# Block list in one packet, masks of a second half on VectorE, split first copies and a new order of steps in a fused attention and MLP kernel

## The chip, the cores and the metric

One core of one Trainium2 chip. The metric is device time in microseconds (us). A profile's span is about 1.8 us shorter than the device time of the same execution. Engines: PE (matrix engine; PEld is its loading of weights), ACT (ScalarE), DVE (VectorE), POOL (GpSimd), SP (issues DMAs). The granted clock is the share of PE's full speed that the profile says it was given.

## The reference

Block-sparse attention (batch 4, 8 heads, 768 positions, head size 64, blocks of 32), then a two-layer MLP with exact gelu on its output:

```python
mask = |blk_i - blk_j| <= 1 or first/last block row or column or sampled_blocks[blk_i]
attn = softmax(where(mask, q k^T / 8, -1e9)) @ v          # per batch and head
x = attn as (3072, 512)
out = gelu(x @ w_in) @ w_out                              # 512 -> 2048 -> 512
```

## The kernel before

The work is cut into eight halves of a batch (384 rows). While the hidden layer and the output of one half run, the scores of the next half are computed in between. What runs when is a string of tokens per stage; each engine executes its part in exactly that order. Stages in time: OPENING (scores of half 1), FIRST (MLP of half 1, scores of half 2), SECOND, SPARSE, DENSE, SPARSE2, and so on.

```python
DENSE = """
H H G t2 u2 H H H M3 t3 u3 H K03 K02 H H O3 S0 O1 K13 K12 C10 L3 O1 C11 O2 D0 W0 S1 O3 D1 O2 W1 S2 O1 X0 K11 O1 E0 O2 C12 D2 E1 W2 S3 ... X2 Y O1 K10 O2 X3 H"""
# H hidden step, O output matmuls, S/W scores and weighted sum of a pair of heads (sparse),
# F/V the same for batch 0, X transposes x for the next hidden layer, I0..I8 small index
# computations on VectorE, t/u transposes of k/q,
# K10: GpSimd gathers the sampled key blocks for the second half of a batch (1), pair 0 of heads;
# C: the same for values,
# L: GpSimd issues four loads, G: VectorE copies of the global value rows
```

Batch 0 is computed densely and masked by a second pair of matmuls, which add -30000 to barred scores:

```python
def first_scores(hb, hp, t, masked=False):
    s1 = sc_pool.tile([P, 2, 512], F32, tag="sc", name="s1")
    c = slice(t, S, NT)
    for l, r_, first_ in ((st["k", hp], st["q", hp], True), (onehot, barred, False)):
        if masked and not first_:
            continue
        for h in range(2):
            pe.matmul(s1[:, h, 0:HALF], lhsT=l[r, c], rhs=r_[r, cq], ...)      # ... cut
    act.activation(pt, s1[:, :, 0:HALF], AF.Exp, scale=scale)
    if masked:          # exists before, but no order used it: token f
        dve.tensor_tensor(pt, pt, mask_t[:, t]..., op=ALU.mult)

def mask_tile(t):       # token m
    pe.matmul(ps[:, 0:HALF], lhsT=onehot[0:64, t:S:NT], rhs=barred[0:64, HALF:S], ...)
    dve.tensor_single_scalar(mask_t[:, t], ps[:, 0:HALF], -1.0, op=ALU.is_gt)
```

The block list is read by a DMA with a partition step of 0, so each of 128 partitions fetches the same 576 bytes:

```python
raw = msk.tile([P, NB, NR, 2], I32, name="raw")
act.dma_start(out=raw, in_=bass.AP(tensor=src, offset=0, ap=[[0, P], [1, NB * NR * 2]]))
```

The softmax here doesn't subtract the row's maximum and nothing guards it: scores larger than these inputs give would overflow.

## Time and profile before

| | before |
|---|---|
| median device time | 293.39 us (292.94 to 294.15, 4 runs) |
| span of the profiled execution | 290.4 us |
| PE busy | 265.4 us, 91% |
| mean granted clock of PE, 11 runs of a later job | 0.987 to 0.994 |

All lines of the page carry L54, a helper, so tiles and not lines tell what an instruction is: hp is the hidden layer, op the output, s scores, kg_all and v_gat gathered keys and values (and, in batch 0, exponentials that borrow their space). Busy time first, page of before:

```profile
PE 265.4 (91%) x3477; PEld 166.6 (57%) x3516; DVE 132.5 (46%) x352; ACT 163.1 (56%) x215; POOL 95.1 (33%) x134
```

PE bounds the kernel. Only its 25 idle us, stretches of low clock and removed matmuls can pay. The windows view of before: a stretch of time, then busy us and instruction count of each engine, the granted PE clock, DMA share, GB/s.

```profile
33.00:72.00 39.00, 36.88 (x395) 21.42 (x400) 26.16 (x113) 25.94 (x33) 6.27 (x14) 1.00 0.77 157
...
182.00:186.00 4.00, 0.10 (x6) 0.01 (x2) 1.31 (x3) 0.67 (x1) 1.18 (x1) 0.98 0.00 0
186.00:188.50 2.50, 2.50 (x29) 1.12 (x29) 0.56 (x1) 1.67 (x3) 0.00 (x0) 0.50 0.00 0
188.50:190.00 1.50, 1.34 (x16) 0.94 (x17) 0.57 (x1) 0.17 (x2) 0.00 (x0) 0.75 0.00 0
```

PE stands for 4 us at 182 us, and then runs at half clock. The timeline of PE in before says what it waited for (start, duration, instruction group, in brackets the idle time before it and what ended it):

```profile
181.75 0.34 PE L54 MATMUL s<-tq,tk 64*128 64x128 bf16 x6
185.99 0.48 PE L54 MATMUL s<-tq,kg_all 64*128 64x32 bf16 x22 [3.90 <-POOL kg_all L54]
186.40 0.50 PE L54 MATMUL s<-tq,kgl 128*128 128x128 bf16 x3
186.70 1.91 PE L54 MATMUL op<-w_out_sb,g 128*128 128x512 bf16 x4
```

Four output matmuls take 1.91 us; four took 1.03 us elsewhere. The timeline of POOL in before shows the other side, the end of gathers and four load issues in one queue from 150 to 186 us:

```profile
166.56 1.65 POOL L54 INDIRECT_COPY v_gat<-v_flat,idx_v 128x1024 f32 x1 [2.00 <-PE od L54]
168.15 0.80 POOL L54 DMA_DIRECT2D st<-in_k_dram  x1
...
176.95 1.18 POOL L54 INDIRECT_COPY kg_all<-tk,idx_k 128x704 f32 x1 [2.08 <-issue]
179.45 1.43 POOL L54 INDIRECT_COPY v_gat<-v_flat,idx_v 128x768 f32 x1 [1.32 <-issue]
184.75 1.18 POOL L54 INDIRECT_COPY kg_all<-tk,idx_k 128x704 f32 x1 [3.87 <-issue]
```

A key gather is busy for 1.2 to 1.6 us but comes only every 3.3 to 4.1 us: ahead of most stand 2 us or more of "issue", time in which POOL waits for nothing that the profile shows. (The profile's notes call spans on POOL rough, so a part of this may be the gather itself.) So a busy share of 33% hides a queue that is full from 150 to 186 us. The last is K10, pair 0's, which is the first that the next half's scores need.

The opening, timeline of ACT in before:

```profile
6.56 0.83 ACT L54 CAST st<-w_out_sb 128x768 bf16<-128x768 f32 x1 [4.09 <-DMA w_out_sb<-in_k_dram]
...
10.85 8.55 ACT L54 ACTIVATE kg_all<-s 128x768 bf16<-128x768 f32 x12 [1.02 <-PE s L54]
...
29.89 1.28 ACT L54 ACT_TABLE_LOAD   x1
```

k's cast waits for k until 6.56 us, the first exponential runs at 10.85 us, and the table load at 29.89 us marks the end of the 24 exponentials.

### The profile page before, as it was taken

The numbers are of one execution on the slowest core, as the hardware profiler recorded it, in microseconds if no ns is written. First come the engines' busy times: TensorE is split into PE (matmuls) and PEld (weight loads), VectorE is DVE, ScalarE is ACT, GpSimd is POOL, SyncE is SP. The second block draws the span as 40 slices with busy tenths as digits, with TensorE's granted clock in tenths as the row PEclk, the third lists the DMA queues.
The fourth block names the chain that finished last, engine by engine and source line by source line (L and its number), as shares of the span: only waits on it lengthen the run. The fifth ranks groups of instructions, "written<-read, shape, count | busy, mean of one in ns | idle before, by whom it ended". The sixth has DMA issues, their size and how long they took to land.

```text
span 290.4 us, 7951 instructions
## 1 busy us (share of the span) xinstructions
PE 265.4 (91%) x3477; PEld 166.6 (57%) x3516; DVE 132.5 (46%) x352; ACT 163.1 (56%) x215; POOL 95.1 (33%) x134
## 2 busy tenths in 40 slices
PE   0899799999999989999999999499999999999995
PEld 0566454565556755565657755266566765665544
DVE  5465585367714653274524730376633560253002
ACT  2698458764467726654576726426358546655520
POOL 8402530013353364352543474132273343100000
PEclk9999999999999999999999999799999999999999
DMA  5999999119970219387751169059100200010102
GB/s 142 266 250 210 213 229 196 50 50 242 218 122 3 74 36 165 57 212 200 164 91 38 38 107 148 0 145 248 60 2 2 74 36 2 2 52 22 40 36 72
DMA packets 30178, 31.34 MB, mean 108 GB/s; under 512 B 13664, under 2 KB 24288, under 8 KB 30144
## 3 DMA queue, kind: packets, MB, share of 16 engines
q0 software_dynamic: 11936, 13.24, 25.8%
q1 hardware_dynamic: 18064, 17.53, 23.2%
q8 instruction: 27, 0.44, 0.6%
q10 hardware_dynamic: 144, 0.07, 0.2%
q14 instruction: 7, 0.06, 0.1%
HBM read 27.34 MB, written 6.29 MB: 116 GB/s over the span
## 4 chain that ended last, share of the span: by engine, by line
PE 81%; ACT 5%; issue 5%; POOL 3%; DVE 3%; DMA 2%; ACTq 0%
PE op L54 26%; PE hp L54 25%; PE s L54 12%; PE og L54 9%; PE ps L54 4%; ACT kg_all L54 2%; PE psx L54 2%; DMA raw<-in_sampled_blocks_dram 2%; ACT g L54 2%; POOL v_gat L54 2%; PE od L54 1%; PE sd L54 1%; DVE pt_all L54 1%; POOL st L54 1%; POOL kg_all L54 1%
## 5 line engine op out<-in xcount | busy, mean ns | idle before, releaser
L54 PE MATMUL op<-w_out_sb,g 128*128 128x512 bf16 (+1 forms) x361 | 90.3, 373 | 2.3 <-issue 0.6
L54 PE MATMUL hp<-xT,w_in_sb 128*128 128x384 bf16 x512 | 88.2, 326 | 4.3 <-ACT g L54 3.8
L54 ACT ACTIVATE g<-hp 128x768 bf16<-128x768 f32 x64 | 51.0, 810 | 61.5 <-PE hp L54 61.4
L54 PEld LDWEIGHTS <-w_in_sb 128*128 128x128 bf16 x512 | 49.1, 98 | 38.2 <-issue 5.5
L54 ACT ACTIVATE pt_all<-s 128x1024 bf16<-128x1024 f32 (+2 forms) x72 | 44.2, 686 | 30.8 <-PE s L54 30.0
L54 PEld LDWEIGHTS <-g 128*128 128x128 bf16 x400 | 35.8, 98 | 29.2 <-issue 3.3
L54 POOL INDIRECT_COPY kg_all<-tk,idx_k 128x704 f32 x24 | 30.2, 1258 | 56.0 <-issue 51.5
L54 DVE TENSOR_TENSOR pt_all<-pt_all,mask_x 128x768 bf16<-128x768 bf16 x24 | 16.0, 667 | 60.1 <-ACT pt_all L54 60.1
L54 POOL INDIRECT_COPY v_gat<-v_flat,idx_v 128x1024 f32 (+1 forms) x18 | 28.6, 1591 | 41.4 <-issue 18.7
L54 PEld LDWEIGHTS <-pt_all 128*32 128x32 bf16 (+2 forms) x840 | 23.9, 101 | 6.8 <-issue 1.5
L54 DVE COPY os<-op 128x512 f32<-128x512 f32 (+1 forms) x25 | 16.6, 666 | 23.1 <-PE op L54 23.1
L54 PE MATMUL s<-tq,tk 64*128 64x128 bf16 (+1 forms) x240 | 25.7, 274 | 0.9 <-DVE tq L54 0.6
L54 PE MATMUL ps<-ident,st 128*64 128x128 bf16 x384 | 17.2, 233 | 8.3 <-ACT st L54 7.4
L54 ACT ACT_TABLE_LOAD x16 | 20.5, 1283 | 5.7 <-PE hp L54 4.2
L54 PEld LDWEIGHTS <-tk 64*128 64x128 bf16 (+1 forms) x312 | 16.2, 104 | 12.6 <-issue 5.8
L54 PEld LDWEIGHTS <-st 128*64 128x64 bf16 x384 | 12.8, 116 | 15.7 <-issue 7.5
L54 ACT ACTIVATE v_gat<-s 128x768 bf16<-128x768 f32 x24 | 18.3, 811 | 5.9 <-PE s L54 5.7
L54 ACT ACTIVATE kg_all<-s 128x768 bf16<-128x768 f32 x24 | 17.6, 819 | 2.8 <-PE s L54 2.7
L54 DVE TENSOR_TENSOR x<-og,rc 128x384 bf16<-128x384 f32 x32 | 17.8, 557 | 1.1
L54 DVE COPY tk<-ps 128x768 bf16<-128x768 bf16 x15 | 14.3, 955 | 8.4 <-PE ps L54 8.1
L54 DVE COPY tq<-ps 128x768 bf16<-128x768 bf16 (+1 forms) x16 | 14.9, 928 | 6.6 <-PE ps L54 4.9
L54 PEld LDWEIGHTS <-kg_all 64*128 64x128 bf16 (+1 forms) x672 | 14.2, 94 | 5.7 <-POOL kg_all L54 4.1
(111 smaller groups left out, 228.5 us busy)
## 6 DMA issues: line engine op xcount, KB each, us to landing
out_dram<-os SPq DMA_DIRECT2D x23, 256.0 KB, 2.3
v_flat<-v_flat SPq DMA_DIRECT2D x6, 594.0 KB, 7.0
st_v<-in_v_dram SPq DMA_DIRECT2D x12, 256.0 KB, 4.8
st<-in_k_dram POOLq DMA_DIRECT2D x7, 384.0 KB, 7.9
st<-in_q_dram POOLq DMA_DIRECT2D x7, 384.0 KB, 9.1
v_flat<-v_flat SPq DMA_DIRECT2D x6, 396.0 KB, 4.8
w_in_sb<-in_moe_w_in_dram POOLq DMA_DIRECT2D x2, 1024.0 KB, 18.0
w_out_sb<-in_moe_w_out_dram POOLq DMA_DIRECT2D x2, 1024.0 KB, 26.2
```

The source lines that it names most:

```text
L54: return self._tc.keep_in_program_order(f(*args, **kwargs))
```

## The change

Its intent: read the block list once and spread it by a matmul with ones; take the mask matmuls of 15 of 24 tiles of half 2 off PE (tokens f and m); let the first pair's copies start earlier; and set the steps in a new order around that. The transposed k of batch 0 is also kept in another order of columns.

```diff
-H H G t2 u2 H H H M3 t3 u3 H K03 K02 H H O3 S0 O1 K13 K12 C10 L3 O1 C11 ... K11 ... C12 ... K10 O2 X3 H
+M3 H H t2 u2 H H H t3 u3 H H H O2 K03 K02 O1 L3 K10 S0 O1 C10 O2 D0 O1 G O1 W0 S1 O1 K12 O2 C11 ... C12 ... K13 ... K11 O1 X1 ...
 (all other orders are rewritten too; in FIRST, m0 to m5 are added and 15 F become f)
-    raw = msk.tile([P, NB, NR, 2], I32, name="raw")
+    raw = msk.tile([1, NB, NR, 2], I32, name="raw")
-    act.dma_start(out=raw, in_=bass.AP(tensor=src, offset=0, ap=[[0, P], [1, NB * NR * 2]]))
+    act.dma_start(out=raw, in_=bass.AP(tensor=src, offset=0, ap=[[0, 1], [1, NB * NR * 2]]))
-    dve.tensor_copy(sbi, raw[:, :, :, 0])
-    dve.tensor_copy(sbf, sbi)
+    dve.tensor_copy(raw_b, raw[:, :, :, 0].rearrange("p n s -> p (n s)"))
+    pe.matmul(ps_raw, lhsT=ones, rhs=raw_b, start=True, stop=True)
+    dve.tensor_copy(sbf.rearrange("p n s -> p (n s)"), ps_raw)
@@ transpose_qk
+        if b == 0 and which == "k":                     # k of batch 0 stays in transposed order
+            to, frm, n = dst.rearrange("p (j n) -> p j n", j=NT), ps, NT
-            transpose_qk(0, hp, w, pair, (act if w == "k" else (act, dve)) if hp == 0 else dve, st)
+            transpose_qk(0, hp, w, pair, (((dve, 0, 1 / 3), (act, 1 / 3, 1)) if w == "k" else ((dve, 0, .5), (act, .5, 1)))
+                         if hp == 0 else dve, st)
```

More of the change, by code (lines that the diff above doesn't have):

```diff
@@ L59 @@
 OPENING = """
-A0 k1 F00 F01 F02 F03 F04 q1 P0 F05 F10 F11 k2 F12 q2 F13 J0 F14 F15 F20 J1 V00 V01 P1 V02 F21 k3 F22 q3 F23 F24 F25 J2 X0 F30 V10 V11 V12 F31 F32 F33 X1 V20 J3 V21 V22 F34 M1 F35 X2 V30 V31 L1 V32 H X3"""
+A0 F00 k1 F01 F02 q1 F03 F04 F05 k3 P0 F10 F11 F12 k2 q2 F13 J0 F14 F15 F20 V00 V01 V02 F21 J1 F22 q3 F23 F24 F25 X0 F30 V10 V11 V12 P1 F31 F32 J2 F33 X1 V20 V21 V22 J3 F34 M1 F35 X2 V30 V31 L1 V32 H X3"""
 FIRST = """
-I0 H H I1 H H I2 H H H I3 O1 I4 H O2 I5 O1 F00 O2 F01 F02 O1 I6 V00 F03 F04 O1 F05 O1 I7 F10 F11 V01 V02 F12 F13 O2 V10 F14 F15 O2 X0 F20 F21 O1 V11 B V12 F22 F23 t0 O1 F24 F25 u0 X1 O1 V20 V21 F30 F31 u1 V22 F32 O2 t1 F33 O2 X2 I8 F34 K00 F35 V30 O1 V31 V32 H Q1 O1 K01 Q0 R X3 O2"""
+H H m0 I0 m1 m2 I1 H H m3 m4 H I2 I3 H H I4 H O2 I5 O1 f00 O2 f01 m5 f02 O2 I6 I7 F03 F04 V00 O1 F05 f10 V01 O1 f11 V02 f12 f13 O2 f14 f15 O1 V10 O1 X0 F20 F21 u0 V11 V12 B F22 F23 V20 O1 t0 f24 f25 O1 X1 V21 O1 f30 F31 u1 V22 F32 O2 t1 f33 F34 O1 V30 f35 K00 X2 O1 I8 O1 V31 V32 Q0 O1 R Q1 H K01 X3 O2"""
@@ L63 @@
 SECOND = """
-H t2 C00 H t3 M2 u3 C01 C02 H K02 K03 u2 H H H H H K10 G O1 C10 O2 S0 C11 O3 L2 C12 O1 D0 W0 S1 E0 O2 K11 O3 K12 D1 X0 W1 S2 E1 O1 X1 O2 D2 O1 W2 S3 O1 X2 O1 E2 D3 O1 W3 E3 O3 Y K13 O1 X3 O1 H"""
+H t2 H u3 t3 C00 H C01 C02 H G H H H M2 H K02 O2 K03 S0 u2 K11 K10 C10 C11 O4 D0 O2 L2 W0 S1 O3 D1 X0 C12 O1 E0 W1 S2 O2 E1 O1 X1 K12 D2 O1 W2 S3 O2 X2 E2 D3 O1 W3 E3 O2 K13 Y X3 O3 H"""
 SPARSE = """
-H H H O1 H H H H B Z H O3 S0 O2 t1 O2 K01 W0 S1 O1 t0 O2 X0 W1 u0 S2 O2 K00 R C00 C01 O1 X1 u1 W2 S3 O1 X2 O1 C02 O4 W3 H O2 X3 O2"""
+H H Z H H B H O1 H H O1 H O2 S0 O1 t1 K01 O3 W0 S1 O1 t0 X0 O2 W1 u0 S2 X1 O1 K00 R O2 C00 O1 C01 C02 u1 W2 S3 O2 X2 O3 W3 H O2 X3 O2"""
@@ L67 @@
 DENSE = """
-H H G t2 u2 H H H M3 t3 u3 H K03 K02 H H O3 S0 O1 K13 K12 C10 L3 O1 C11 O2 D0 W0 S1 O3 D1 O2 W1 S2 O1 X0 K11 O1 E0 O2 C12 D2 E1 W2 S3 O1 X1 O1 E2 D3 O1 W3 E3 O2 X2 Y O1 K10 O2 X3 H"""
+M3 H H t2 u2 H H H t3 u3 H H H O2 K03 K02 O1 L3 K10 S0 O1 C10 O2 D0 O1 G O1 W0 S1 O1 K12 O2 C11 D1 O1 X0 W1 C12 S2 O2 E0 K13 O1 D2 O1 E1 W2 S3 O1 K11 O1 X1 E2 D3 O1 W3 E3 O2 Y X2 O3 X3 H"""
 SPARSE2 = """
-H H H O1 H H H H B Z H O3 S0 O2 t1 O2 K01 W0 S1 O1 t0 O2 X0 W1 u0 S2 O2 K00 R C00 C01 O1 X1 u1 W2 S3 O1 X2 O1 C02 O4 W3 H O2 X3 O2"""
+H H Z H H B H O1 H H O1 H O2 S0 O1 t1 K01 O3 W0 S1 O1 t0 X0 O2 W1 u0 S2 X1 O1 K00 R O2 C00 O1 C01 C02 u1 W2 S3 O2 X2 O3 W3 H O2 X3 O2"""
@@ L71 @@
 DENSE2 = """
-H H G t2 u2 H H H t3 u3 H K03 K02 H H O3 S0 O1 K13 K12 C10 O1 C11 O2 D0 W0 S1 O3 D1 O2 W1 S2 O1 X0 K11 O1 E0 O2 C12 D2 E1 W2 S3 O1 X1 O1 E2 D3 O1 W3 E3 O2 X2 Y O1 K10 O2 X3 H"""
+H H t2 u2 H H H t3 u3 H H H O2 K03 K02 O1 K10 S0 O1 C10 O2 D0 O1 G O1 W0 S1 O1 K12 O2 C11 D1 O1 X0 W1 C12 S2 O2 E0 K13 O1 D2 O1 E1 W2 S3 O1 K11 O1 X1 E2 D3 O1 W3 E3 O2 Y X2 O3 X3 H"""
 LAST_SPARSE = """
-H H H H H H H H O3 S0 O5 W0 S1 O5 W1 S2 O1 X0 O2 Z X1 O1 W2 S3 O1 X2 O4 W3 H X3 O2"""
+H H H Z H O1 H H H H O2 S0 O5 S1 W0 O5 W1 S2 O1 X0 X1 O3 W2 S3 O4 X2 O1 W3 H X3 O2"""
@@ L75 @@
 LAST = """
-H H H H O2 H O1 H H H O29"""
+H H H O2 H H O2 H H H O28"""
 ORDERS = (OPENING, FIRST, SECOND, SPARSE, DENSE, SPARSE2, DENSE2, LAST_SPARSE, LAST)
@@ L173 @@
     ident = small("ident", [P], BF16, const)
+    ones = msk.tile([1, P], BF16, name="ones")
+    raw_b = msk.tile([1, NB * NR], BF16, name="raw_b")
     part_i = small("part_i", [1], I32)
@@ L176 @@
     dve.memset(ident, 0.0)
+    dve.memset(ones, 1.0)
     pool.iota(part_i, pattern=[[0, 1]], base=0, channel_multiplier=1)
@@ L216 @@
     hit = small("hit", [NB, NR])
-    dve.tensor_copy(sbi, raw[:, :, :, 0])
-    dve.tensor_copy(sbf, sbi)
+    dve.tensor_copy(raw_b, raw[:, :, :, 0].rearrange("p n s -> p (n s)"))
+    ps_raw = mm_pool.tile([P, NB * NR], F32, tag="mm", name="ps_raw")
+    pe.matmul(ps_raw, lhsT=ones, rhs=raw_b, start=True, stop=True)
+    dve.tensor_copy(sbf.rearrange("p n s -> p (n s)"), ps_raw)
     dve.tensor_scalar(hit, sbf, key_b[:, 0:1], None, op0=ALU.is_equal)
@@ L263, in gather_constants @@
     def gather_constants():
+        dve.tensor_copy(sbi, sbf)
         for n, (m, op) in enumerate(((15, ALU.bitwise_and), (7, ALU.bitwise_and),
@@ L418, in transpose_qk @@
                 pe.transpose(ps[64 * h:64 * h + 64, j, :], pair[:, h, j * D:j * D + D], ident)
-        engs = eng if isinstance(eng, tuple) else (eng,)
-        n = P // len(engs)
-        for i, e in enumerate(engs):
-            cast(e, dst.rearrange("p (n j) -> p n j", j=NT)[:, n * i:n * i + n],
-                 ps.rearrange("p j n -> p n j")[:, n * i:n * i + n])
+        if b == 0 and which == "k":
+            to, frm, n = dst.rearrange("p (j n) -> p j n", j=NT), ps, NT
+        else:
+            to, frm, n = dst.rearrange("p (n j) -> p n j", j=NT), ps.rearrange("p j n -> p n j"), P
+        for e, lo, hi in eng if isinstance(eng, tuple) else ((eng, 0, 1),):
+            c = slice(int(lo * n), int(hi * n))
+            cast(e, to[:, c], frm[:, c])
         st[which, hp] = dst
@@ L545, in first_scores @@
                 r = slice(64 * h, 64 * h + 64)
-                pe.matmul(s1[:, h, 0:HALF], lhsT=l[r, c], rhs=r_[r, cq],
+                pe.matmul(s1[:, h, 0:HALF], lhsT=l[r, t * P:t * P + P] if first_ else l[r, c], rhs=r_[r, cq],
                           start=first_, stop=masked or not first_)
```

## The prediction

> **What bounds the kernel now.** The matrix engine: busy 265 of 290.4 us (the page's first part), 81% of the chain that ended last. Only its ~25 idle us and removed matmuls are worth anything. From its waits and the windows by stage:
>
> - Opening, 0 to 33 us: 7.4 us until the first transposes (ScalarE's cast of k), then ScalarE-bound: 24 exponentials from 10.85 to 29.9 us, only ~1 us more than their summed time.
> - 33 to 72 us (hidden layer of the first half, scores of the second): matrix engine 36.9 of 39 us, VectorE 26.2.
> - 182 to 186 us: one 3.9 us wait of scores for GpSimd's last key gather; GpSimd ran ten gathers and four DMA issues in a row from 150 to 186 us. The granted clock was then 0.50 for 2.5 us and 0.75 for 1.5 us: ~1.6 us more. The Trainium skill, "TensorE: Matmul & The Clock Gate", section "What's actually happening", says half rate follows an idle window of about 3.4 us; this trace agrees. Together ~5.5 us.
>
> **What the change does.**
>
> 1. Block list: 1 partition, not 128. It landed at 5.6 us; the mask work then held VectorE to 7.7 us, and q's cast began at 7.76. But q itself lands only at 7.5 us. Gain ~0.2 us, up to 0.5 more if 128 fewer packets let k and q land earlier.
> 2. Split copies: VectorE's half of q began 0.04 us after ScalarE's ended. The Trainium skill, "PSUM — Partial Sum Buffer", section "PSUM bank collisions raise a hardware error", forbids sharing a bank; the trace agrees: halves are serial. But the first scores need only k's first third and q's first half, both now VectorE's: ~0.2 us earlier. Opening: -0.5 us.
> 3. Masks by VectorE for 15 of 24 tiles of the second half: removes 15 pairs of 384-column matmuls (0.165 us a pair, start to start), adds 6 (~0.16): -1.5 us of matrix work. VectorE gains 15 multiplies (0.52 each, as the later mask multiplies) and 6 compares from PSUM (~0.5): ~11 us, so ~38 us of work in a stage of ~38. From the first masked tile I sum 26 us of in-order VectorE work, ending at 72.5 to 73.5 us, hardly before the old end (73.7). Gain 0 to 0.7 us.
> 4. Order of gathers: the key gather of pair 0, last of ten before, becomes third; last is now pair 1's, needed ~4 us later. The GpSimd chain stays ~36 us, ending ~186, when the matrix engine asks for it (~185.5 to 187). The wait shrinks to 0 to 0.8 us, the clock dip goes: -5 us, the main gain.
> 5. Other reorderings: -0.4 us; the stages already run the matrix engine at 97 to 99%.
>
> Sum: about -6.8 us: 286.6 us, 8 times in 10 within 283.5 to 289.5. Chances: faster by over 2% 0.6, within 2% 0.37, slower 0.03.
>
> **What the profile would show.** First exponential at 10.0 to 10.6 us. VectorE near 95% busy from 45 to 70 us, with matrix waits for VectorE of masked tiles or x, 1 to 3 us in total; the third half's scores start less than 2 us earlier. No wait over 1 us for GpSimd near 180 us and no clock below 0.9 there; the hidden stage of batch 2's first half ~29 us long, as batch 1's, not 35.
>
> **What would make it wrong.** If pair 1's gather is a few us late, the wait only moves to the next scores: 288 to 291. If multiplies lose speed to GpSimd (one took 1.7 us instead of 0.56), the second half comes 2 to 4 us later. If VectorE keeps up better than summed, 1 to 2 us more are gained.

## The result and the profile after

288.78 us median (288.23 to 289.13, 4 runs) against 293.39 us: 4.6 us less. The ratio is 0.9839 (95% interval 0.9812 to 0.9865). All ratios here are the mean time of one kernel's fast runs over that of the other's fast runs of the same rounds, so not quite the ratio of the medians quoted. The interval lies clear of 1. The two profiled executions differ by less than the medians: their spans are 290.4 and 286.8 us. The kernel before varies together with its mean clock: of its 31 runs in the later jobs, the 8 with a clock below 0.99 took 293.9 us on average, the other 23 (0.992 to 0.994) took 292.7; a longer dip in clock may be why, but no profile of them was kept. The profiled execution, 292.2 us at 0.994, is one of the short ones.

The table loads of ACT mark the end of a run of exponentials or gelus; they show where time was won and lost (starts in us, the two profiled executions):

| table load after | before | after | after minus before |
|---|---|---|---|
| exponentials of half 1 (opening) | 29.89 | 29.63 | -0.26 |
| exponentials of half 2 (FIRST) | 74.62 | 75.29 | +0.67 |
| exponentials of half 3 (SECOND) | 102.22 | 102.74 | +0.52 |
| exponentials of half 4 (SPARSE) | 133.12 | 133.21 | +0.09 |
| exponentials of half 5 (DENSE) | 165.64 | 165.46 | -0.18 |
| gelus of half 5 | 181.39 | 181.75 | +0.36 |
| exponentials of half 6 (SPARSE2) | 201.46 | 197.20 | -4.26 |
| exponentials of half 7 (DENSE2) | 233.97 | 230.16 | -3.81 |
| exponentials of half 8 (LAST_SPARSE) | 263.14 | 259.55 | -3.59 |
| end of span | 290.4 | 286.8 | -3.6 |

In these two executions the changed kernel has won nothing until 181 us; between 181 and 201 us it wins all of it at once. The same views as before. Busy times, page of after:

```profile
PE 265.4 (93%) x3453; PEld 163.5 (57%) x3495; DVE 142.0 (50%) x375; ACT 162.5 (57%) x215; POOL 95.1 (33%) x134
```

PE is as busy as before: from 31 to 75 us, where the masks are, it is 1.0 us less busy, and in the first 31 us 1.5 us more, by longer matmuls in the opening. Windows of after:

```profile
33.00:72.00 39.00, 37.46 (x378) 19.83 (x382) 33.98 (x131) 25.78 (x33) 8.52 (x17) 1.00 0.74 152
...
182.00:186.00 4.00, 3.87 (x83) 2.24 (x76) 1.90 (x3) 2.88 (x4) 1.55 (x2) 1.00 0.01 2
186.00:188.50 2.50, 1.57 (x42) 1.17 (x44) 0.86 (x3) 1.02 (x2) 1.14 (x3) 1.00 0.30 111
```

The 4 us at 182 are work now, and the clock stays at 1.00. Timelines of PE and then of POOL in after:

```profile
181.86 0.43 PE L54 MATMUL s<-tq,kg_all 64*128 64x32 bf16 x22
...
186.78 0.44 PE L54 MATMUL s<-tq,kg_all 64*128 64x32 bf16 x22 [0.86 <-POOL kg_all L54]
```

```profile
162.91 1.18 POOL L54 INDIRECT_COPY kg_all<-tk,idx_k 128x704 f32 x1 [2.10 <-issue]
...
185.54 1.18 POOL L54 INDIRECT_COPY kg_all<-tk,idx_k 128x704 f32 x1 [2.45 <-issue]
```

Pair 0's keys are there at 164 us, 18 us before their use. The queue as a whole is no faster, it ends at 186.7 us; its last gather is now pair 1's, and PE waits 0.86 us for it.

In the stage from 33 to 72 us, DVE went from 26.2 to 34.0 us busy. The chain of waits of after in that stage (start, us, what):

```profile
62.46 0.97 DVE kg_all L54 x2
...
68.86 0.59 DVE v_gat L54
69.45 0.27 DVE xT L54
69.72 0.18 DVE own L54
...
72.74 0.19 DVE idx_v L54
72.93 0.11 DVE rc L54
...
73.06 0.57 DVE x L54
73.63 0.05 issue
73.68 0.34 PE psx L54 x3
```

The same chain in before ran through PE alone from 60 us on:

```profile
70.06 0.74 PE og L54 x24
70.80 1.95 PE hp L54 x12
...
73.35 0.86 PE op L54 x4
```

Now it runs through DVE: multiplies (kg_all, v_gat), then the small index work of I8 (own to idx_v, 69.7 to 72.9 us), then the last x. PE's waits in after say what that costs, and what else is new:

```profile
PE psx L54 <- DVE x L54: 1.4, 1, 1.4
...
PE og L54 <- DVE vgl L54: 1.0, 2, 0.9
```

The wait for vgl is for G, which the new order puts just ahead of W0 in the dense stages. The opening, timeline of ACT in after:

```profile
3.74 0.83 ACT L54 CAST st<-w_out_sb 128x768 bf16<-128x768 f32 x1 [1.18 <-DMA w_out_sb<-in_k_dram]
...
9.22 0.81 ACT L54 ACTIVATE kg_all<-s 128x768 bf16<-128x768 f32 x1 [0.40 <-PE s L54]
10.76 1.51 ACT L54 ACTIVATE kg_all<-s 128x768 bf16<-128x768 f32 x2 [0.73 <-PE s L54]
12.94 2.21 ACT L54 ACTIVATE kg_all<-s 128x768 bf16<-128x768 f32 x3 [0.67 <-PE s L54]
...
29.63 1.28 ACT L54 ACT_TABLE_LOAD   x1
```

k is there 2.8 us earlier, the first exponential runs 1.6 us earlier, and the last ends 0.3 us earlier: ACT waits for PE in between. A part is lost already ahead of the first exponential: k's transposes end at 5.5 us, but VectorE, still at the mask work and q's cast, begins its third of the copy only at 6.73 us, and ACT waits 2.46 us for it. And the 0.3 us are uncertain: in the profile of before_gather (below), whose code is the same up to DENSE, before's opening ends at 30.93 us and not at 29.89.

### The profile page after: what moved, and what is told of

Same layout as the page of the kernel before. It is cut to its first block, busy times and chain, and to the rows that moved or that the text cites. A ratio compares the mean times of both kernels' runs of the same rounds, so it can differ in the third digit from the quotient of the medians.

```text
span 286.8 us, 7929 instructions
## 1 busy us (share of the span) xinstructions
PE 265.4 (93%) x3453; PEld 163.5 (57%) x3495; DVE 142.0 (50%) x375; ACT 162.5 (57%) x215; POOL 95.1 (33%) x134
## 4 chain that ended last, share of the span: by engine, by line
PE 60%; DVE 16%; issue 11%; POOL 7%; ACT 5%; POOLq 0%; DVEq 0%; ACTq 0%
PE hp L54 21%; PE op L54 18%; PE s L54 7%; PE og L54 6%; PE ps L54 4%; POOL kg_all L54 3%; POOL v_gat L54 2%; DVE v_flat L54 2%; PE psx L54 2%; DVE v_gat L54 1%; ACT L54 1%; ACT g L54 1%; POOL st L54 1%; PE od L54 1%; ACT kg_all L54 1%
## 5 line engine op out<-in xcount | busy, mean ns | idle before, releaser
L54 DVE TENSOR_TENSOR pt_all<-pt_all,mask_x 128x768 bf16<-128x768 bf16 x24 | 14.7, 614 | 56.5 <-ACT pt_all L54 56.5
L54 PEld LDWEIGHTS <-pt_all 128*32 128x32 bf16 (+2 forms) x818 | 22.0, 99 | 9.0 <-issue 2.9
L54 PE MATMUL s<-tq,tk 64*128 64x128 bf16 (+1 forms) x240 | 24.6, 272 | 1.2 <-DVE tq L54 0.7
L54 PEld LDWEIGHTS <-tk 64*128 64x128 bf16 (+1 forms) x312 | 14.1, 96 | 14.0 <-issue 9.0
L54 DVE COPY tk<-ps 128x768 bf16<-128x768 bf16 (+1 forms) x16 | 13.4, 835 | 11.3 <-PE ps L54 11.2
L54 DVE CAST v_flat<-st_v 128x1536 bf16<-128x1536 f32 (+1 forms) x10 | 8.9, 917 | 17.4 <-POOL v_gat L54 17.4
```

The costliest lines, as they stand in the source:

```text
L54: return self._tc.keep_in_program_order(f(*args, **kwargs))
```

## The experiments

Theory: the gather order alone is the net gain; the masks on VectorE and the early opening give nothing or cost. Rival: the gain is a sum of all parts. Twelve kernels ran, in three jobs (the third on another chip); all gave correct results. The kernel before, run beside them, had medians of 293.16, 292.83 and 292.80 us. The change itself was not run in these jobs: each comparison with it is one across jobs, in which before's median moved from 293.39 down to 292.80 us. So a difference of medians of 0.6 us or less says nothing. "By the ratios" below means the difference of the two ratios to before, times 293 us, which takes this drift out.

| kernel | median us (range, runs) | ratio to before (95% interval) |
|---|---|---|
| after (the change) | 288.78 (288.23 to 289.13, 4) | 0.9839 (0.9812 to 0.9865) |
| before_gather | 286.99 (286.61 to 287.47, 4) | 0.9781 (0.9732 to 0.9831) |
| after_oldgather | 292.59 (291.99 to 293.64, 4) | 0.9986 (0.9933 to 1.0039) |
| after_pemask | 287.15 (286.83 to 287.69, 6) | 0.9796 (0.9758 to 0.9835) |
| after_raw128 | 290.35 (289.42 to 291.36, 6) | 0.9899 (0.9858 to 0.9940) |
| after_i8late | 288.08 (287.65 to 289.06, 6) | 0.9838 (0.9808 to 0.9869) |
| after_k11 | 287.37 (286.81 to 288.40, 6) | 0.9811 (0.9780 to 0.9841) |
| after_gearly | 287.35 (287.07 to 287.63, 6) | 0.9805 (0.9776 to 0.9833) |
| after_open3 | 288.23 (286.50 to 289.09, 6) | 0.9826 (0.9791 to 0.9861) |
| best | 285.35 (285.29 to 286.11, 5) | 0.9757 (0.9735 to 0.9780) |
| dvemask_relieved | 286.31 (285.57 to 286.66, 5) | 0.9774 (0.9751 to 0.9796) |
| extra_rows, extra_same | 288.29, 288.81 (1 each, state unknown) | |

### before_gather: one swap on the kernel before

```diff
 DENSE (of before)
-... O3 S0 O1 K13 K12 C10 L3 ... X2 Y O1 K10 O2 X3 H
+... O3 S0 O1 K10 K12 C10 L3 ... X2 Y O1 K13 O2 X3 H
```

> The kernel before with one edit: in the DENSE order the key gather of pair 0 (K10) and that of pair 3 (K13) trade places, so that pair 0's comes third and not last. Theory (the net gain of the change is the gather order alone): the 3.9 us wait of the matrix engine for GpSimd near 182 us and the clock of 0.5 after it are gone; time 287.5 to 289.5, that is 4 to 6 us below before, as fast as the whole change. Rival (the gain is a sum over opening, masks and gathers): 290.5 to 292, a part of the 4.6 us only.

286.99 us: below even the range expected, and 1.8 us below the whole change (1.7 by the ratios; the two intervals overlap a little, the single runs do not). The clock stays at 1.00, and PE's timeline there has no wait:

```profile
182.83 0.34 PE L54 MATMUL s<-tq,tk 64*128 64x128 bf16 x6
183.01 0.43 PE L54 MATMUL s<-tq,kg_all 64*128 64x32 bf16 x22
```

Two tokens that trade places give at least what the whole change does, and probably more. So the rest of the change, the late place of pair 1's gather included, most likely costs time. The profiles say where: from table load to table load, the change is 1.3 us ahead of this run in the opening, and loses 0.9 us in FIRST, 1.7 in SPARSE2 and 0.4 in DENSE2.

### after_oldgather: the change with the old DENSE order

```diff
-DENSE of after
+DENSE of before
```

> The changed kernel with the DENSE order of the kernel before put back. Theory (gather order alone): the long wait near 182 us is back, with the low clock; time 293 to 294.5, no faster than before. Rival (sum over the parts): 290.5 to 292.5, since opening and masks keep their share.

292.59 us, ratio 0.9986, interval around 1: without its gather order the change gains nothing that can be told from noise. The median is 0.4 us below the range expected and 0.6 us below before in the same job, so a gain of some tenths from the other parts isn't excluded. PE waits 4.18 us for kg_all until 185.81 us. The mean granted clock of the profiled execution is 0.994, that of before, and 0.91 between 180 and 200 us: the dip is back.

```profile
180.00:200.00 20.00, 15.82 (x304) 9.70 (x302) 10.91 (x18) 8.05 (x12) 5.25 (x10) 0.91 0.41 103
```

This edit puts the whole DENSE order back, G, M3, L3 and the places of H and O too, so it undoes more than the gathers; that the gathers suffice is shown by before_gather.

### after_pemask: masks on the matrix engine again

```diff
 FIRST (of after): every f -> F, tokens m0 to m5 removed
```

> The changed kernel with every masked tile of the second half masked by the matrix engine again (F for f in the FIRST order, no mask tiles). Theory (VectorE full from 34 to 73 us turns the saved matmuls into a wait): matrix work grows by about 1.5 us, VectorE loses 11 us, the 1.4 us wait for x at 73 us goes; time within 1 us of the changed kernel, 287.8 to 289.3. Rival (the masks on VectorE pay for themselves): 290 to 291.5.

287.15 us: 1.6 us faster than the change (1.3 by the ratios, intervals overlapping), beyond the range expected.

```profile
33.00:72.00 39.00, 37.73 (x405) 20.54 (x404) 26.13 (x110) 26.02 (x33) 8.20 (x17) 1.00 0.78 159
```

```profile
72.84 0.34 PE L54 MATMUL psx<-ident,x 128*128 128x128 bf16 x3 [0.53 <-DVE x L54]
```

DVE is 26.1 us busy from 33 to 72 us (34.0 in after), the wait for x at 73 us falls from 1.43 to 0.53 us, and the stage is 0.6 us shorter by its table loads (45.06 against 45.66 us), though PE does more. Another 0.8 us of the profiled difference lie in DENSE2, where after waits 0.87 us for vgl and this run didn't; that wait hangs on tenths of timing. How it stands without that is the matter of the last two kernels.

### after_raw128: the block list to 128 partitions again

```diff
-    raw = msk.tile([1, ...]); DMA with ap=[[0, 1], ...]; ones matmul
+    raw = msk.tile([P, ...]); DMA with ap=[[0, P], ...]; casts to sbi and sbf
```

> The changed kernel with the block list read to 128 partitions again and cast to int32 and fp32 from there; order and split copies as changed. Theory: the 128 small packets are what held back k and q at the start, so k's cast on ScalarE starts again at 6 to 6.8 us (3.7 with one packet) and the first exponential at 10.3 to 11 us (9.2); the opening ends 0.5 to 1.5 us later and the time grows by 0.3 to 1.5 us. Rival 1 (k and q landed early for another reason, as the run's own DMA timing): k's cast stays near 3.7 us. Rival 2 (the opening's gain is lost in it anyway): first exponential as said, but the time within 0.3 us of the changed kernel.

290.35 us, 1.6 us slower than the change (1.8 by the ratios). k's cast starts at 6.69 us (3.74 in after), the first exponential at 11.58 us, and the opening ends at 31.71 us, 2.1 us later. So the single packet is worth about 1.6 us in this kernel. The theory holds in kind, and all but k's cast came out larger than it said: the first exponential by 0.6 us, the end of the opening by 0.6, the time by a little. Both rivals fall. It also suggests that the rest of the new opening costs: with the old block list it ends at 31.71 us, and before's own opening ended at 29.89 and, with identical code in the profile of before_gather, at 30.93 us. That is one execution of this kernel against two that differ by 1.0 us, so it is not shown.

### extra_rows and extra_same: are 128 small packets slow, or 128 reads of the same bytes?

```diff
+    extra = msk.tile([P, NB * NR * 2], F32, name="extra")
+    act.dma_start(out=extra, in_=bass.AP(tensor=v.tensor, offset=0, ap=[[192, P], [1, NB * NR * 2]]))  # extra_same: [[0, P], ...]
     act.dma_start(out=raw, ...)
```

> The changed kernel with one more DMA ahead of the block list, never read: 128 packets of 576 bytes, each from a row of its own of v. Theory A (128 small packets ahead of k and q hold them back): k's cast on ScalarE starts at 6 us or later, as with the block list to 128 partitions (6.7), not at 3.7. Theory B (it is 128 reads of the same 576 bytes that are slow): k's cast stays below 4.5 us.

> As extra_rows, but all 128 packets read the same 576 bytes of v. Theory A and theory B both: k's cast at 6 us or later. If it stays below 4.5 us, neither: then it is the block list's own tensor or its place.

ACT's cast of k, first in extra_rows, then in extra_same:

```profile
4.43 0.83 ACT L54 CAST st<-w_out_sb 128x768 bf16<-128x768 f32 x1 [1.39 <-DMA w_out_sb<-in_k_dram]
```

```profile
6.97 0.83 ACT L54 CAST st<-w_out_sb 128x768 bf16<-128x768 f32 x1 [3.92 <-DMA w_out_sb<-in_k_dram]
```

The landing of the extra DMA, again first in extra_rows, then in extra_same (KB, us from issue to landing):

```profile
extra<-in_v_dram ACTq DMA_DIRECT2D x1, 72.0 KB, 2.9
```

```profile
extra<-in_v_dram ACTq DMA_DIRECT2D x1, 72.0 KB, 5.5
```

As many packets of the same size put off k's cast by 0.7 us if each reads its own row, and by 3.2 us if all read the same 576 bytes. k's load, issued by SP at the same 0.74 us, landed after 3.7 and 6.2 us (3.0 in after). Theory B holds: it is the repeated read that is slow, and k's load lands late with it. One execution each, but the difference is of the size seen between before and after, and after_raw128 repeats it. Why repeated reads of the same bytes are slow isn't shown. Nor do these two runs show the worth in time: in extra_same the opening ends 1.5 us later than in extra_rows (31.17 against 29.62), the whole run 0.5 us.

### after_i8late: the index work out of the way

```diff
 FIRST:  ... K00 X2 O1 - I8 - O1 V31 V32 ...
 SECOND: H t2 H u3 t3 + I8 + C00 H ...
```

> The changed kernel, VectorE masks kept, with the last index computation (I8, 2.6 to 3.2 us of small VectorE work that stands just ahead of the last x of the second half) moved behind the next half's transposes. Theory (VectorE's in-order queue, not the masks' data path, is what delays the third half): the 1.4 us wait for x at 73 us goes, the table load near 75.3 us comes 1.2 to 1.6 us earlier, time 287.0 to 288.0. Rival (GpSimd's gathers, started at the same 68 us, hold the next stage anyway): the wait goes but time stays 288.4 to 289.2, with a new wait for v_gat or kg_all between 86 and 92 us.

Both are partly right. The wait for x is gone and the table load at 75.29 comes at 73.44 us, 1.85 us earlier. But 0.3 us of that are an earlier opening, and at the end of SECOND (102.01 against 102.74 us) 0.7 us are left. In between PE waits for POOL:

```profile
89.57 0.30 PE L54 MATMUL og<-v_gat,pt_all 128*32 128x65 bf16 x14 [0.32 <-POOL v_gat L54]
...
96.99 0.49 PE L54 MATMUL sd<-qgl,tk 128*128 128x128 bf16 x6 [0.46 <-POOL qgl L54]
```

PE also waits 1.2 us for vgl in this run (1.0 in after). 288.08 us, 0.7 us below the change by medians, with nearly the same ratio (0.9838): no clear gain. Behind VectorE's queue stands GpSimd's.

### after_k11, after_gearly: the two small waits

```diff
 after_k11, DENSE:     K13 <-> K11
 after_gearly, DENSE and DENSE2: "H H t2" -> "H H G t2", G removed ahead of W0
```

> The changed kernel with the key gathers of pairs 1 and 3 traded in the DENSE order, so that pair 3's is the last of the ten. Theory: the 0.9 us wait for kg_all near 186 us goes and nothing takes its place; time 287.6 to 288.4. Rival (the ten gathers are too slow in any order, so the wait moves to pair 3's scores): a wait of 0.3 us or more for kg_all near 194 us, time 288.4 to 289.2.

> The changed kernel with the copies of the global value rows (G) back at the start of the two dense halves, as before. Theory: the waits for vgl at 153 us (0.16) and 218 us (0.87) go; time 287.6 to 288.2. Rival (G early delays the copies of the transposes, which is why the change moved it): a new wait of 0.5 us or more for tk or tq near 140 and 205 us, time unchanged within 0.4 us.

287.37 and 287.35 us, 1.4 us below the change each by medians, a little under the ranges expected. In both cases the theory holds: the wait named is gone (kg_all near 186 us; vgl at 153 and 218 us) and none above 0.2 us took its place there. The larger of the waits for vgl was this one in after:

```profile
218.00 0.33 PE L54 MATMUL og<-vgl,pt_all 128*128 128x130 bf16 x3 [0.87 <-DVE vgl L54]
```

By the ratios each gained about the wait itself: 0.8 us for a wait of 0.86, 1.0 for waits of 1.03 (the intervals overlap that of the change). For after_k11 about 0.5 us of the profiled gain lie in DENSE2, where nothing was edited: the wait for vgl, whose size changes with timing from run to run. In after_open3's profile it was 1.33 us in DENSE, against 0.16 in after.

### after_open3: scores ahead of transposes in the opening

```diff
-A0 F00 k1 F01 F02 q1 F03 ...
+A0 F00 F01 F02 k1 q1 F03 ...
```

> The changed kernel with three tiles of scores ahead of the second pair's transposes in the opening. Theory (the 1.6 us that the first exponential gains is lost because ScalarE then waits for transposes[...]): ScalarE's waits of 0.73 and 0.67 us after the first and third exponential go or shrink, the exponentials end 0.8 to 1.4 us earlier, near 28.4 us, and the time is 287.4 to 288.2. Rival (the slow first 10 us of the matrix engine cap the opening in any order): the waits move to the next tiles, the end stays within 0.4 us of 29.6 and the time within 0.4 us.

By the trace the rival is right. ACT's waits of 0.73 and 0.67 us become one of 1.25 us, and the exponentials end at 29.27 us (29.63 in after), not near 28.4. The time doesn't decide: 288.23 us, 0.55 below the change by medians and 0.4 by the ratios, with the widest range of the kernels from the change (286.50 to 289.09). This order of the first tiles isn't what limits the opening.

### best and dvemask_relieved: the parts together

```diff
 best:             after_pemask + after_k11 + after_gearly
 dvemask_relieved: VectorE's masks kept, after_i8late + after_k11 + after_gearly
```

> The changed kernel with three edits at once: masks of the second half on the matrix engine again (no f, no m), key gathers of pairs 1 and 3 traded in DENSE, G early in both dense halves. One-packet block list and split copies stay. If the three parts add as measured singly (-1.6, -1.4 and -1.4 us against the change): 284 to 285.2. Rival (they share one slack, GpSimd's gathers): 285.8 to 287, no better than the gather trade on the kernel before (287.0).

> The changed kernel with VectorE's masks kept, I8 late, gathers of pairs 1 and 3 traded, G early. If the masks on VectorE are worth their 1.5 us of matrix work once VectorE's queue is relieved: 284 to 285.2, no slower than the kernel with matrix masks of the same job. Rival (GpSimd's gathers then hold the third half, as the waits at 89 and 97 us showed with I8 late alone): 285.5 to 287, 0.5 to 2 us slower than that kernel.

best: 285.35 us, 0.15 us above the range expected for adding up and below the rival's. It is faster than before (interval 0.9735 to 0.9780) and than the change (0.9812 to 0.9865), since the intervals don't touch. The single gains against the change sum to 4.4 us of medians and 3.4 us came (3.1 and 2.4 by the ratios): after_pemask and after_k11 had both counted a part of the wait for vgl. Against before_gather, which ran in another job and on another chip, the intervals overlap; that best beats the simple swap (1.6 us by medians, 0.7 by the ratios) is likely but not shown.

dvemask_relieved: 286.31 us, 1 us slower than best in the same rounds by medians (0.65 by means, and the single runs overlap), as the rival said. With VectorE's queue relieved, PE waits for POOL again: 0.31 us for v_gat, 0.45 for qgl, 0.6 for kg_all. These waits sum to about 1.4 us, about what the masks save PE (1.5 us in the prediction). So VectorE's masks didn't pay in either setting; how much they cost is known only to some tenths.

## Why the prediction was right or wrong

The total was right: 286.6 predicted with 283.5 to 289.5, and 288.78 measured. It was 2.2 us too low, and the outcome "faster by over 2%", held the likeliest, narrowly did not come. The mechanism of the main term was right, and the terms of the sum were these:

1. "The wait shrinks to 0 to 0.8 us, the clock dip goes: -5 us, the main gain": right. The wait went from 3.90 to 0.86 us, the clock from 0.50 to 1.00, and between the table loads at 165 and 201 us 4.1 us were won. before_gather and after_oldgather show from both sides that this is the gain. The trade alone wins more in that stage: 5.8 us in before_gather, where no wait is left. The stage told to become ~29 us took 35.8 in before, 31.7 in after and 30.0 in before_gather, by its table loads. That the GpSimd queue "stays ~36 us, ending ~186" was read from before's own gather spacing; it ended at 186.7; PE asked for it at 185.9, inside the range told, and so had to wait.
2. Block list, "gain ~0.2 us, up to 0.5 more if 128 fewer packets let k and q land earlier": mis-sized. k's cast came 2.8 us earlier, and undoing it costs 1.6 us. The packets were counted by their bytes and number; what made them slow was that all read the same bytes (extra_same against extra_rows).
3. Opening, "-0.5 us": -0.26 us in the profiles, for other reasons than given. The first exponential came at 9.22 us, earlier than the 10.0 to 10.6 told, and 1.4 us of it was lost again in ACT's waits for PE. PE's pairs of score matmuls took 0.53 us until 13.7 us, and 0.33 us afterwards; in before the change of pace came at 11.6 us. Starting earlier seems to have bought more of the slow stretch; no run separates that. That the opening came out near its figure was partly luck: the block list was worth more than told, and something else in the new opening probably took much of it back (after_raw128). The halves of a copy were serial as told: ACT's two thirds of k began at 7.03 us, when DVE's third ended.
4. Masks on VectorE, "gain 0 to 0.7 us": the mechanism was right and the sign wrong. The chain of waits does run through DVE, which I had summed to end at 72.5 to 73.5 us; its last x ended at 73.6 us, after a wait of 1.43 us. From the opening's end the stage grew by 0.9 us, and after_pemask shows the masks themselves to be a loss. That VectorE would be near 95% busy from 45 to 70 us was close: 22.3 of 25 us. The multiplies did not slow: the 14 that the profile shows took 0.56 us on average.
5. Other reorderings, "-0.4 us": half of it. From table load to table load SECOND, SPARSE and DENSE became shorter by 0.15, 0.43 and 0.27 us, DENSE2 and LAST_SPARSE longer by 0.45 and 0.22: -0.2 us together. Without the new wait for vgl, 1.0 us in the profile, it would have been about -1.2; after_gearly removes that wait. The order of VectorE's copies ahead of W0 was seen in the diff and not costed.

In the two profiled executions the sum is -4.1 (term 1), -0.3 (terms 2 and 3), +0.9 (term 4) and -0.2 us (term 5): -3.6. The medians differ by 4.6; the missing 1 us is the profiled execution of before, 1.2 us under its median, and if its opening was a short one (29.89 against 30.93 us in before_gather), terms 2 and 3 won more than 0.3 us. The step that failed is term 4: its chain on VectorE ended at 73.6 us, close to the sum, but PE needed the last x 1.43 us sooner, and the stage grew by 0.9 us instead of shrinking.

## What to carry to other kernels

Look first for the one long wait of the bounding engine and ask whether the instruction it waits for could simply stand earlier in its own queue: here two exchanged tokens gave at least as much as a rewrite of three mechanisms. An engine with a low busy share can still be the full one, if its instructions have dead time ahead of them; count the spacing of instructions, not their busy time. Work taken off the bounding engine did not pay here, because the engine that took it over had no room in its queue at that very place, ahead of what the bounding engine needs next; ask for that room first.

## What the Trainium skill lacked or had wrong

- "DMA: Bandwidth & Descriptors" (sections on small descriptors and on latency) has nothing on many descriptors that read the same bytes. Here 128 packets of 576 bytes landed 2.9 us after issue when each read its own row, and 5.5 us when all read the same bytes, and k's load, issued beside them, landed after 3.7 and 6.2 us.
- "TensorE: Matmul & The Clock Gate", section "What's actually happening": half rate after about 3.4 us idle agrees (clock 0.50 after a wait of 3.90 us). Its warm-up after one busy window of about 3.4 us fits before (slow from 7.4 to about 11.6 us), and after less well: scores run from 8.36 us on, and the pairs stay at 0.53 us until 13.7 us, 5.3 us. The page also says that its window is free-running; whether that makes up the difference isn't shown. And the profile's clock column shows 1.00 through this whole stretch, so either it misses this, and the matmuls' durations have to be read, or the slow pairs have another cause.
- "PSUM — Partial Sum Buffer", section "PSUM bank collisions raise a hardware error": agrees as far as this shows; copies of one bank by two engines stood one behind the other in both kernels (in after ACT's at 7.03 us after DVE's at 6.73 us, 0.27 us long). Whether the program's own waits did that isn't shown.
- "VectorE: DVE Perf Modes", section "Why PSUM operands drop a tier", caps a bf16 copy from PSUM at two elements a cycle. This case shows what layout does within that cap: with k kept in the transposed order the copy of 768 columns took 0.56 us, and q's, whose columns are permuted, 0.95 to 0.96 us in the same opening. Nothing is lacking: the page itself ties that rate to elements that lie side by side.
- "GPSIMD Engine Reference" gives no cost for starting a gather. Here most indirect copies of 1.2 to 1.7 us had 1.3 to 4.1 us ahead of them in which POOL waited for nothing that the profile shows; what that time is stays open.
